# A transformer block's feed-forward layer: the last two of four batch elements with seven block products for eight in the first layer

## The chip, the cores and the metric

The kernel runs on one core of a Trainium2 chip. The metric is device time in microseconds, the median of three runs. The engines are TensorE (PE, with its weight loads as PEld), the vector engine (DVE), the scalar engine (ACT), GpSimd (POOL) and SyncE (SP), which issues all the DMAs here.

## The reference

Attention over chunks of 32 queries, each with its neighbours (16 to the left, 8 to the right) and 8 memory cells, then a feed-forward layer with a squared relu:

```python
for c in range(S // 32):                       # q, k, v: (4, 8, 768, 64)
    k_full, v_full = [mem_k, k[l:r]], [mem_v, v[l:r]]
    a = softmax(q_c @ k_full.T / sqrt(64))
    out[:, :, c] = a @ v_full
x = out.transpose(0, 2, 1, 3).reshape(3072, 512)
h = x @ w_in                                   # 512 x 2048
g = s * relu(h) ** 2 + b
y = g @ w_out                                  # 2048 x 512
```

All data are fp32, and w_in and w_out arrive as 64-bit words that the kernel rebuilds into fp32.

## The kernel before

The 3072 tokens are eight chunks of 384, two to a batch element (`NCHUNK`, `HALVES`). The 2048 hidden features are 16 slices of 128. A step `u` is one chunk with one slice (`STEPS`, line 100); there are 128. Chunks 0 and 1 share the first 32 steps, while the weights arrive; each later chunk has 16 steps of its own, and from step 40 on steps go in pairs.

Every operand of the two layers is held as a high and a low part of fp32r, and a product is three matmuls (high by low, low by high, high by high). `hidden` (line 720) makes a step of the first layer: 4 slices of the 512 input channels by 3 matmuls of 384 columns into one PSUM bank. Four scalar-engine passes follow in that bank: relu (736), square (737), affine with s and b (738) and the rounding to the high part (739); the vector engine subtracts it for the low part (740). `result` (line 743) makes a step of the second layer: three token tiles, three matmuls of 512 columns each (751), into three accumulator banks that a chunk holds for all its steps. The last step of a chunk copies them out (772, 774), and `ends` (781) does that for the last chunk, its last tile in two halves.

`attend(ch, d)` (539) makes attention for one half of a chunk's heads: loads (555, 562), scores (574), maximum, difference, exponential and sum (482 to 493), normalisation on POOL (500), transposes of 32 x 32 blocks on the vector engine (531, 32 to a half), products with v (588), and x's high and low parts (597, 598). From chunk 2 on, the values of one visit go on PE with the scores of the next, as one chain of instructions, for which four PSUM banks must be free.

`weight` (676) rebuilds one slice of w_in or w_out from a staging buffer of the ring `words` and splits it. All weights stay in SBUF afterwards: slices 0 to 7 in tiles of their own, 8 to 15 in tiles shared with the two layers' parts.

The order of all instructions is laid out before the run, by `Plan.lay` (201): each operation has a priority in step numbers (`anchor`, `H_AT`, `R_AT`, `FETCH`), a holding time (`HOLD`), and rings of buffers and banks (`Ring`, `room`, line 414) that it needs. Each engine then serves its list in this order, and waits by semaphores where an operand is late. `lock` keeps marked operations of the vector engine and POOL apart in that layout.

Of the kernel before, what the change touches and what calls it, by code (L numbers as in the profile page):

```python
# [60 lines left out]
BEFORE = 4.0  # L61
# [19 lines left out]
POOLED = set()  # L81
BANKS = 8
# [11 lines left out]
def G_AT(i, a):  # L94
# [4 lines left out]
PARTS = [0, 4, 10, NF]  # L99
STEPS = ([(ch, f) for lo, hi in zip(PARTS, PARTS[1:]) for ch in range(2) for f in range(lo, hi)]  # L100
         + [(ch, f) for ch in range(2, NCHUNK) for f in range(NF)])
FIRST = {}
for _u, (_, _f) in enumerate(STEPS):
# [8 lines left out]
            small=235, part=290, wide=1040, tiny=200, norm6=1000, norm3=650, mul6=470, mul3=270, issue=440)  # L112
# [4 lines left out]
CODE = dict(hidden=6, result=6, half=6, first=96, scores=96, value1=64, value2=32, scores1=96, scores2=96, turn=2, value=32)  # L117
# [55 lines left out]
class Plan:  # L173
# [27 lines left out]
    def lay(self, warm=None):  # L201
# [33 lines left out]
        while todo:  # L235
# [6 lines left out]
            for e in engines:  # L242
# [10 lines left out]
                put, got = [], None  # L253

                soon = min(((y[2].prio, y[1], y[0]) for y in waiting[e] if y[0] <= t + SOON[e]), default=None) if SOON[e] else None
                while ready[e]:
                    x = heapq.heappop(ready[e])
                    o = x[2]
                    if soon and soon[:2] < x[:2]:
                        put.append(x)  # L260
                        heapq.heappush(events, soon[2])
                        break
                    if e in pin and pin[e] is not o:
                        put.append(x)
                        continue
                    new = [v for v in o.vals if v.slot is None and v.ring.tiles is not None]
                    other = "POOL" if e == "DVE" else "DVE"
                    held = o.lock and e in lock and lock[other] > t

                    if o.lock and e in lock and free[other] <= t and any(y[2].lock and y[:2] < x[:2] for y in ready[other]):  # L270
                        put.append(x)
                        continue
                    given = []
                    for v in new if not held else ():
                        if not v.ring.can(v):
                            break
# [68 lines left out]
def body(ctx: ExitStack, tc: tile.TileContext, qkv, w1, w2, out):  # L345
# [30 lines left out]
    for i in range(NEARLY):  # L376
        early_tiles.append(at(WEIGHT_AT(0, 0), [P, SLOT], F32, name=f"early{i}", tag=f"slot{i}"))
        if i < 4:
            stat_tiles.append(tuple(at(top[0] % TURN_B, [QB, 2 * GB], F32, name=f"{n}{i}") for n in ("top", "den", "rden")))

    def weight_tile(half, f):
        late = f >= LATE_F
        if late and f not in wts:
            wts[f] = const.tile([P, SLOT], F32R, name=f"ww{f}", tag=f"slot{f - LATE_F}")
        if not late and (half, f) not in wts:
            place(WEIGHT_AT(half, f), 8 * DM)
            wts[half, f] = const.tile([P, 2, DM], F32R, name=f"w{half}_{f}", tag=f"w{half}_{f}")
        if not late:
            return wts[half, f]
        lo = half * (2 * DM + WEIGHT_AT(1, f) // 4)  # L390
        return wts[f][:, lo:lo + 2 * DM].rearrange("p (a n) -> p a n", a=2)

    xr = [[at(X_AT(i, a, d), [P, 2 * TOK], F32R, name=f"x{'HL'[a]}{d}_{i}") for a in range(2) for d in range(2)] for i in range(2)]
    gs = Ring([tuple(at(G_AT(i, a), [P, TOK], F32R, name=f"g{'HL'[a]}{i}") for a in range(2)) for i in range(3)])
    for half in range(2):
        for f in range(NF):
            weight_tile(half, f) if f < LATE_F else None
# [5 lines left out]
    words = ring("words", 3, [P, 2 * DM], F32)  # L403
    raws = ring("raw", 2, [P, QK], F32)
# [5 lines left out]
    outs = ring("partial", 2 * NT, [P, DM], F32)  # L410

    spare = [BANKS - 1]

    def room(r, kind):
        n = r.live.get
        if kind == "acc":
            r.free += spare
            spare.clear()
            return n("acc", 0) < NT
        few = sum(n(k, 0) for k in "stvSV")  # L420
        if kind in "SV":
            return few < 5 and r.next.get("v", 0) == len(r.vals["v"])
        if kind in "stv":
            return few < FEW if not r.next.get("acc", 0) else few < 3
        return n("h", 0) < 2
# [31 lines left out]
    def anchor(ch, d):  # L457
# [5 lines left out]
        return starts[ch] - JOIN - (8.0 if ch > NALONE else APART) * (2 - d)  # L463
# [3 lines left out]
    def xt(x, a, c):  # L467
        return x.tile[2 * a + c // 2][:, c % 2 * TOK:(c % 2 + 1) * TOK]
# [70 lines left out]
    def attend(ch, d):  # L539
# [5 lines left out]
        due = a + 2 if alone else anchor(ch, 2) if d else anchor(ch, 1)  # L545
# [32 lines left out]
        if d == 0:  # L578
            x_vals[ch] = Val(x_ring)
        x = x_vals[ch]  # L580
# [9 lines left out]
        def store(V):  # L590
            at = due + 0.9 if alone else due - 4
            for r in range(2):
                lo, hi = (0, 4 * QB) if r == 0 else (4 * QB, 6 * QB)
                to = lambda a, lo=lo, hi=hi: x.tile[2 * a + d][:, lo:hi]
# [22 lines left out]
        def soft(S):  # L617
            for n in range(2):
# [5 lines left out]
                if early:  # L624
                    turn(late, t, y, lambda m: t.parts.values(), (ch, d, n))
                else:
                    flip(a + BEFORE + n, t, y)
# [115 lines left out]
    def result(u):  # L743
# [3 lines left out]
        last = u + 1 == len(STEPS) or STEPS[u + 1][0] != ch  # L747

# [5 lines left out]
        for t in range(NT):  # L754
# [3 lines left out]
            if u + 1 == len(STEPS):  # L758
                ends(u, t, acc, products, (g["H"], g["L"], w["H"], w["L"]))
                continue  # L760
# [4 lines left out]
            if f < NF - 1 and o is None:  # L765
# [9 lines left out]
            if f < NF - 1:  # L775
                continue
# [4 lines left out]
    def ends(u, t, acc, products, reads):  # L781

        row = STEPS[u][0] * TOK + t * P
        cols = (0, DM) if t + 1 < NT else (0, DM // 2, DM)
        for i, (lo, hi) in enumerate(zip(cols, cols[1:])):
            o = Val(outs)
            op("PE", "result" if hi - lo == DM else "half", R_AT(u), lambda lo=lo, hi=hi: products(acc, t, lo, hi), (*reads, acc[0]), (acc[lo],))
            if (t + i) % 2:
                op("DVE", "out", u, lambda o=o, lo=lo, hi=hi: nc.vector.tensor_copy(o.tile[:, lo:hi], acc.tile[:, lo:hi]), (acc[lo],), (o[0],))
# [10 lines left out]
    for u, (ch, f) in enumerate(STEPS):  # L800
        if u == starts[ch]:
            plan.group = None
            for y in (ch, 0), (ch, 1), (ch + 1, 0):
                if y not in made and (y[0] == ch or NALONE <= ch < NCHUNK - 1):
                    made.add(y)
                    attend(*y)
            if ch == NCHUNK - 1:
                last_[3]()
        hidden(u)
        result(u)  # L810

    laid = plan.lay(warm)
    with tc.manual_schedule():
# [40 lines left out]
```

## Time and profile before

| | |
|---|---|
| runs | 601.72, 601.75, 602.56 us; median 601.75 |
| profiled execution, first to last instruction | 600.1 us; no other time is given for it |
| PE busy | 591.2 us (99%), 5052 instructions |
| weight loads busy | 528.9 us (88%) |
| vector engine busy | 333.5 us (56%) |
| scalar engine busy | 347.4 us (58%) |
| POOL busy | 24.2 us (4%) |
| HBM | 48.24 MB read, 6.29 MB written |

Busy time is the union of an engine's instructions. Matmuls overlap in the array and their ends are modelled, so the pace of a group is read from the starts of the groups, not from one matmul's duration. The profile's chain is found backward from the last instruction: at each step to what released it, or to the instruction before it on its engine.

### The profile page before, as it was taken

The page shows a single profiled execution, that of the slowest core. Times are in us where ns is not written, and L with a number is a line of the kernel's source. Part 1 is how long each engine was busy: PE and PEld are TensorE (multiplying, and loading weights), DVE is VectorE, ACT ScalarE, POOL GpSimd, SP SyncE. Part 2 cuts the span into 40 slices and gives each one's busy share as a digit, 9 for nine tenths or more (in the row PEclk, how much of TensorE's full clock was granted, in tenths as well). Part 3 has the DMA queues.
Part 4 walks back from the last instruction along what each step waited for, and adds up shares of the span by engine and source line. Part 5 has one row for each costly group of instructions (what it writes and reads, how often), then busy time and mean ns, then how long its engine had stood idle before and what let it go on. Part 6 is the DMA issues. An engine that isn't in the chain of part 4 may idle for free.

```text
span 600.1 us, 12337 instructions
## 1 busy us (share of the span) xinstructions
PE 591.2 (99%) x5052; PEld 528.9 (88%) x5057; DVE 333.5 (56%) x916; ACT 347.4 (58%) x743; POOL 24.2 (4%) x36
## 2 busy tenths in 40 slices
PE   8989999999999999999999999999999999999997
PEld 4778999989999999989989998998989989999996
DVE  4998999997381734728266371744628265121111
ACT  6999988855455546446445455546446545544553
POOL 1000000010010100001000010100001010000000
PEclk9999999999999999999999999999999999999999
DMA  8966644431230403103031210413013110010001
GB/s 341 416 237 217 196 147 168 143 134 53 68 118 1 134 0 131 55 13 121 0 133 54 73 61 1 133 54 131 2 31 114 42 56 1 1 52 1 0 2 53
DMA packets 17481, 55.32 MB, mean 92 GB/s; under 512 B 1936, under 2 KB 2192, under 8 KB 17424
## 3 DMA queue, kind: packets, MB, share of 16 engines
q1 hardware_dynamic: 17424, 54.53, 25.9%
q8 instruction: 39, 0.64, 0.4%
q14 instruction: 18, 0.15, 0.1%
HBM read 48.24 MB, written 6.29 MB: 91 GB/s over the span
## 4 chain that ended last, share of the span: by engine, by line
PE 93%; ACT 3%; DVE 2%; DMA 1%; issue 0%; SPq 0%; ACTq 0%
PE ps L728 44%; PE ps L751 43%; PE ps L588 4%; PE ps L574 3%; ACT t L486 1%; DMA early<-qkv 1%; DVE xL L598 0%; PE ps L516 0%; DVE wv L710 0%; ACT aT L525 0%; DVE t L498 0%; ACT wv L699 0%; DVE w L715 0%; ACT ps L738 0%; ACT w L705 0%
## 5 line engine op out<-in xcount | busy, mean ns | idle before, releaser
L740 DVE TENSOR_TENSOR gL<-ps,gH 128x384 fp32r<-128x384 f32 x128 | 71.2, 556 | 206.0 <-ACT gH L739 204.8
L736 ACT ACTIVATE ps<-ps 128x384 f32<-128x384 f32 x128 | 61.3, 479 | 173.7 <-PE ps L728 173.5
L728 PE MATMUL ps<-xH,w 128*128 128x384 f32 x512 | 130.5, 336 | 0.0
L728 PE MATMUL ps<-xH,ww 128*128 128x384 f32 x512 | 130.5, 336 | 0.0
L751 PE MATMUL ps<-ww,gH 128*128 128x512 f32 (+1 forms) x386 | 118.5, 389 | 0.0
L751 PE MATMUL ps<-w,gH 128*128 128x512 f32 x384 | 118.5, 390 | 0.0
L531 DVE STREAM_TRANSPOSE aT<-t 32x96 f32<-32x96 f32 x384 | 103.5, 270 | 6.1
L728 PEld LDWEIGHTS ps<-xH,ww 128*128 128x128 f32 x512 | 92.6, 188 | 1.3
L728 PEld LDWEIGHTS ps<-xH,w 128*128 128x128 f32 x512 | 92.7, 188 | 1.2
L728 PE MATMUL ps<-xL,w 128*128 128x384 f32 x256 | 87.2, 341 | 0.0
L728 PE MATMUL ps<-xL,ww 128*128 128x384 f32 x256 | 86.7, 339 | 0.0
L738 ACT ACTIVATE ps<-ps,b_sb,s_sb 128x384 f32<-128x384 f32 x128 | 82.5, 644 | 4.2
L751 PEld LDWEIGHTS ps<-ww,gH 128*128 128x128 f32 x386 | 72.4, 188 | 13.6
L751 PEld LDWEIGHTS ps<-w,gH 128*128 128x128 f32 x384 | 72.1, 188 | 13.6
L751 PE MATMUL ps<-w,gL 128*128 128x512 f32 x192 | 75.7, 394 | 0.8 <-DVE gL L740 0.8
L751 PE MATMUL ps<-ww,gL 128*128 128x512 f32 (+1 forms) x193 | 75.3, 390 | 0.0
L739 ACT ACTIVATE gH<-ps 128x384 fp32r<-128x384 f32 x128 | 62.9, 492 | 4.0
L737 ACT ACTIVATE ps<-ps 128x384 f32<-128x384 f32 x128 | 60.8, 475 | 4.1
L728 PEld LDWEIGHTS ps<-xL,w 128*128 128x128 f32 x256 | 48.2, 188 | 2.1
L728 PEld LDWEIGHTS ps<-xL,ww 128*128 128x128 f32 x256 | 48.2, 188 | 1.9
L751 PEld LDWEIGHTS ps<-w,gL 128*128 128x128 f32 x192 | 36.1, 188 | 7.7 <-DVE gL L740 1.5
L751 PEld LDWEIGHTS ps<-ww,gL 128*128 128x128 f32 x193 | 36.3, 188 | 6.2
(57 smaller groups left out, 415.1 us busy)
## 6 DMA issues: line engine op xcount, KB each, us to landing
raw<-qkv SPq DMA_DIRECT2D x28, 576.0 KB, 6.7
words<-w SPq DMA_DIRECT2D x24, 512.0 KB, 3.6
v<-qkv SPq DMA_DIRECT2D x28, 384.0 KB, 3.8
out<-partial SPq DMA_DIRECT2D x23, 256.0 KB, 2.0
early<-w SPq DMA_DIRECT2D x8, 512.0 KB, 10.2
early<-qkv SPq DMA_DIRECT2D x3, 576.0 KB, 6.1
early<-qkv SPq DMA_DIRECT2D x4, 384.0 KB, 9.7
early<-qkv SPq DMA_DIRECT2D x1, 577.0 KB, 3.6
```

Of the source, the lines that this page charges most:

```text
L486: op("ACT", "part", late + 0.2, lambda m=m: nc.scalar.activation(tv()[:, m, :], sv()[:, m, :], AF.Exp, bias=top()[:, m:m + 1], scale=SCALE ...
L531: nc.vector.transpose(aT.tile[rows, :, c, r * CHUNK:(r + 1) * CHUNK], t.tile[c * CHUNK:(c + 1) * CHUNK, r::2, g * CHUNK:(g + 1) * CHUNK])
L574: nc.tensor.matmul(S[n].tile[c * CHUNK:(c + 1) * CHUNK, (at * GB + j) * CELL:(at * GB + j + 1) * CELL], raw.tile[rows, k * CHUNK:(k + 1) * ...
L588: nc.tensor.matmul(to, vals_[half].tile[:, at:at + D], aT[n].tile[:, m, c, :], start=True, stop=True)
L728: nc.tensor.matmul(h.tile[:, :TOK], weight_tile(0, f)[:, wi, c * P:(c + 1) * P], xt(x, xi, c), start=(c == 0 and n == 0), stop=(c == NC_T ...
L736: op("ACT", "relu", u, lambda: nc.scalar.activation(hp(), hp(), AF.Relu), (), (h[0],))
L737: op("ACT", "square", u, lambda: nc.scalar.activation(hp(), hp(), AF.Square), (), (h[0],))
L738: op("ACT", "affine", u, lambda: nc.scalar.activation(hp(), hp(), AF.Identity, scale=s_sb, bias=b_sb), (c_s[0], c_b[0]), (h[0],))
L739: op("ACT", "high", u, lambda: nc.scalar.activation(g.tile[0], hp(), AF.Copy), (h[0],), (g["H"],))
L740: op("DVE", "low", u, lambda: nc.vector.tensor_tensor(g.tile[1], hp(), g.tile[0].bitcast(F32), ALU.subtract), (h[0], g["H"]), (g["L"],))
L751: nc.tensor.matmul(acc.tile[:, lo:hi], g.tile[gi][:, t * P:(t + 1) * P], weight_tile(1, f)[:, wi, lo:hi], start=(first and n == 0), stop=( ...
```

## The change

The steps of chunks 0 to 3 (elements 0 and 1) stay, 64 of them; the slices of chunk 3 go in another order (`LATER_F`). Elements 2 and 3 are made in 16 units (`unit`, `second`), eight to an element. A unit takes both token halves and two slices of the hidden features. Tokens, input channels and features are each cut in two, and the eight block products of the first layer become seven (`prod`), by the form of Strassen's scheme with shared sums. For it there are

- sums of the four parked x blocks (`sums`, `splits`): the attention of elements 2 and 3 leaves x in fp32 in four buffers (`park`, two scalar-engine copies a half in place of the split), three further sums and differences are made from them with one more buffer, and seven operands of 768 columns are split into high and low parts. They lie where slices 0 to 2, 6 and 7 of w_in and the two x tiles lay;
- mixed blocks of w_in (`mix`): for each of eight pairs of slices three operations of 512 and three of 256 columns, on the vector engine or, for pairs 1 and 3, POOL, then two splits of 512 columns and four writes to HBM. They have dates from step 30.82 to 61.59, and take the staging ring;
- loads of these blocks (`fetch`): 512 KB three times a unit and once every two units, into seven buffers that slices 8 to 14 of w_in held;
- the sums behind the products: three banks (kind L) take the products, of which one is used by products 0, 2, 4 and 6 in turn. Two of its states and one of another bank are saved by the scalar engine to SBUF; the vector engine adds them to a later bank (`hadd`) and squares the positive part (`hsq`); affine and high part stay on the scalar engine, the low part on the vector engine, now from SBUF;
- the second layer in two ways: the first token half accumulates in three banks over the eight units, the second half in banks of one unit each (kind r) that the vector engine adds to an SBUF buffer (`accum`).

The visits of attention for chunks 4 to 7 have dates of their own (`VISITS`), the transposes too (`FLIPS`). While a visit waits for its banks, no new bank of kind L or r is given out (`kept`).

```diff
+MIX = [30.82, 32.64, 34.69, 47.24, 47.55, 47.83, 61.59, 43.54]
+MIXENG = ['DVE', 'POOL', 'DVE', 'POOL', 'DVE', 'DVE', 'DVE', 'DVE']
+XENG = ['DVE', 'POOL', 'DVE', 'DVE']
+AHEAD = 0.88
+FLIPS = [5.12, 6.59, 6.68, 6.21, 6.01, 5.03, 6.84, 2.85, 10.89, 4.12, 6.97, 6.28]
+PROD = [-1.21, 1.4, 1.6, 1.68, 2.1, 3.33, 3.43]
+CHAIN = {'11': 2.04, '22': 0.52, '12': 3.22, '21': 4.37}
+SECONDS = [2.94, 3.55, 8.0, 3.91]
+XSUM = [-0.96, -0.62, 1.09, -0.07]
+XSPLIT = [-6.05, -2.28, -0.26, -2.49, 0.78, 0.92, -0.32]
+RBANKS = 2
...
 
 PARTS = [0, 4, 10, NF]
+NPLAIN = 2
+LATER_F = [3, 4, 5, 0, 1, 2, *range(6, NF)]
 STEPS = ([(ch, f) for lo, hi in zip(PARTS, PARTS[1:]) for ch in range(2) for f in range(lo, hi)]
-         + [(ch, f) for ch in range(2, NCHUNK) for f in range(NF)])
+         + [(2, f) for f in range(NF)] + [(3, f) for f in LATER_F])
+NPAIR = NF // 2
+NUNIT = (B - NPLAIN) * NPAIR
+UNIT = 3.75
+VISITS = [41.16, 48.0, 50.14, 54.14, 58.95, 69.41, 72.68, 81.06, 85.03]
+TURNED = set()
...
                     new = [v for v in o.vals if v.slot is None and v.ring.tiles is not None]
+                    if kept and any(v.kind in ("L", "r") for v in new):
+                        put.append(x)
+                        continue
                     other = "POOL" if e == "DVE" else "DVE"
                     held = o.lock and e in lock and lock[other] > t
...
+        if kind == "L":
+            return n("L", 0) < 3
+        if kind == "r":
+            return n("r", 0) < (RBANKS if r.next.get("r", 0) < len(r.vals["r"]) - NT else NT)
...
+    def sums(b):
+
+        at = AT(NPAIR * (b - NPLAIN))
+        plan.group = ("x", b)
+        full = lambda i: [c_park[i][r] for r in range(2)]
+        tt = lambda e, to, p, q, o: e.tensor_tensor(park(to), park(p), park(q), o)
+        firsts.append((b, 7, wide_op(XENG[0], "pre", at + XSUM[0], lambda e: tt(e, 4, 2, 3, ALU.add), (*full(2), *full(3)), full(4))))
+        wide_op(XENG[1], "pre", at + XSUM[1], lambda e: tt(e, 2, 0, 2, ALU.subtract), full(0), full(2))
+        splits(b, 0, 0, at + XSPLIT[0])
+        splits(b, 1, 1, at + XSPLIT[1])
+        wide_op(XENG[2], "pre", at + XSUM[2], lambda e: tt(e, 0, 4, 0, ALU.subtract), full(4), full(0))
+        splits(b, 2, 0, at + XSPLIT[2])
+        wide_op(XENG[3], "pre", at + XSUM[3], lambda e: tt(e, 1, 1, 0, ALU.subtract), full(0), full(1))
+        splits(b, 3, 4, at + XSPLIT[3])
+        splits(b, 4, 2, at + XSPLIT[4])
+        splits(b, 5, 1, at + XSPLIT[5])
+        splits(b, 6, 3, at + XSPLIT[6])
+
+    def splits(b, i, p, at):
+        src = [c_park[p][r] for r in range(2)]
+        firsts.append((b, i, op("ACT", "khigh", at, lambda: nc.scalar.activation(operand(i, 0), park(p), AF.Copy), src, (c_x[i]["H"],))))
+        firsts.append((b, i, op("DVE", "klow", at, lambda: nc.vector.tensor_tensor(operand(i, 1), park(p), operand(i, 0).bitcast(F32), ALU.subtract),
+                                (*src, c_x[i]["H"]), (c_x[i]["L"],), lock=True)))
...
+    def mix(j):
+
+        f1, f2 = 2 * j, 2 * j + 1
+        at = MIX[j]
+        plan.group = ("mix", j)
...
+        m = Val(words, "mix")
+        part = lambda lo, hi: m.tile[:, lo * DM // 2:hi * DM // 2]
+        two = lambda f, a: plain(f)[:, a, :].bitcast(F32)
+        e = MIXENG[j]
+        wide_op(e, "mix2", at, lambda e: e.tensor_tensor(part(0, 2), two(f2, 0), two(f2, 1), ALU.add), (w2v["H"], w2v["L"]), (m[0], m[1]))
+        wide_op(e, "mix2", at, lambda e: e.tensor_tensor(part(2, 4), two(f1, 0), two(f1, 1), ALU.add), (w1v["H"], w1v["L"]), (m[2], m[3]))
+        wide_op(e, "mix2", at, lambda e: e.tensor_tensor(part(2, 4), part(0, 2), part(2, 4), ALU.subtract), (m[0], m[1]), (m[2], m[3]))
+        wide_op(e, "mix1", at, lambda e: e.tensor_tensor(part(0, 1), part(1, 2), part(0, 1), ALU.subtract), (m[1],), (m[0],))
+        wide_op(e, "mix1", at, lambda e: e.tensor_tensor(part(1, 2), part(1, 2), part(2, 3), ALU.subtract), (m[2],), (m[1],))
+        wide_op(e, "mix1", at, lambda e: e.tensor_tensor(part(3, 4), part(2, 3), part(3, 4), ALU.subtract), (m[2],), (m[3],))
+        for h in range(2):
+            v = Val(words, "stage")
+            to = lambda a, v=v: v.tile.bitcast(F32R).rearrange("p (m a n) -> p a m n", m=2, a=2)[:, a]
+            fro = lambda h=h: m.tile.rearrange("p (m n) -> p m n", m=4)[:, (1, 0)[h]:(3, 4)[h]:(1, 3)[h], :]
+            need = [m[1], m[2]] if h == 0 else [m[0], m[3]]
+            op("ACT", "thigh", at, lambda to=to, fro=fro: nc.scalar.activation(to(0), fro(), AF.Copy), need, (v["H"],))
+            op("DVE", "tlow", at, lambda to=to, fro=fro: nc.vector.tensor_tensor(to(1), fro(), to(0).bitcast(F32), ALU.subtract), (*need, v["H"]), (v["L"],), lock=True)
+            op("SP", "issue", at, lambda v=v, h=h: nc.sync.dma_start(d_mixed[j][h].bitcast(F32), v.tile), (v["H"], v["L"]), (c_mixed[j][h][0],), size=P * TW * 4)
...
+    def fetch(k):
+
+        j, at = k % NPAIR, AT(k) - AHEAD
+        plan.group = ("fetch", k)
+        got = {}
+
...
+        load("mixed0", lambda: d_mixed[j][0], (c_mixed[j][0][0],), at + 1.1)
+        load("mixed1", lambda: d_mixed[j][1], (c_mixed[j][1][0],), at + 2.2)
+        if j % 2 == 0:
+            load("last", lambda: d_last[j // 2].rearrange("p a n -> p (a n)"), (c_last[j][0], c_last[j + 1][0]), at + 2.75)
+        else:
+            got["last"] = c_flow[k - 1]["last"]
...
+        def prod(i, bank, prio, start):
+            v, w = block(k, i)
+
+            def fn():
+                for c in range(2):
+                    for n, (wi, xi) in enumerate(((0, 1), (1, 0), (0, 0))):
+                        nc.tensor.matmul(bank.tile[:, :TOK], w(wi)[:, c * P:(c + 1) * P], operand(i, xi)[:, c * TOK:(c + 1) * TOK],
+                                         start=start and c == 0 and n == 0, stop=start and c == 1 and n == 2, skip_group_check=not start)
+
+            op("PE", "prod", at + prio, fn, (c_x[i]["H"], c_x[i]["L"], v[0]), (bank[0],))
+
+        def save(bank, prio):
+            v = Val(saves)
+            op("ACT", "save", at + prio, lambda: nc.scalar.activation(v.tile, bank.tile[:, :TOK], AF.Copy), (bank[0],), (v[0],))
+            return v
+
+        def chain(name, prio, bank, add):
+            h, g = Val(hs), Val(gs)
+            if add is None:
+                op("ACT", "hrelu", at + prio, lambda: nc.scalar.activation(h.tile, bank.tile[:, :TOK], AF.Relu), (bank[0],), (h[0],))
+                op("ACT", "hsquare", at + prio, lambda: nc.scalar.activation(h.tile, h.tile, AF.Square), (), (h[0],))
             else:
-                op("ACT", "store", u, lambda o=o, lo=lo, hi=hi: nc.scalar.activation(o.tile[:, lo:hi], acc.tile[:, lo:hi], AF.Copy), (acc[lo],), (o[0],))
-            op("SP", "issue", u, lambda o=o, lo=lo, hi=hi: nc.sync.dma_start(out[row:row + P, lo:hi], o.tile[:, lo:hi]), (o[0],), (), size=P * (hi - lo) * 4)
-
+                op("DVE", "hadd", at + prio, lambda: nc.vector.tensor_tensor(h.tile, bank.tile[:, :TOK], add.tile, ALU.add), (bank[0], add[0]), (h[0],))
+                op("DVE", "hsq", at + prio, lambda: nc.vector.scalar_tensor_tensor(h.tile, h.tile, 0.0, h.tile, ALU.max, ALU.mult), (), (h[0],), lock=True)
+            op("ACT", "haffine", at + prio, lambda: nc.scalar.activation(h.tile, h.tile, AF.Identity, scale=s_sb, bias=b_sb), (c_s[0], c_b[0]), (h[0],))
+            op("ACT", "hhigh", at + prio, lambda: nc.scalar.activation(g.tile[0], h.tile, AF.Copy), (h[0],), (g["H"],))
+            op("DVE", "hlow", at + prio, lambda: nc.vector.tensor_tensor(g.tile[1], h.tile, g.tile[0].bitcast(F32), ALU.subtract), (h[0], g["H"]), (g["L"],), lock=True)
+            return g
+
+        A = Val(ps, "L")
+        prod(0, A, PROD[0], True)
+        s1 = save(A, 0.1)
+        Bk = Val(ps, "L")
+        prod(1, Bk, PROD[1], True)
+        g11 = chain("11", CHAIN["11"], Bk, s1)
+        prod(2, A, PROD[2], False)
+        s2 = save(A, 1.2)
+        C = Val(ps, "L")
+        prod(3, C, PROD[3], True)
+        s5 = save(C, 1.7)
+        prod(4, A, PROD[4], False)
+        g22 = chain("22", CHAIN["22"], A, s5)
+        prod(5, C, PROD[5], False)
+        g12 = chain("12", CHAIN["12"], C, s2)
+        prod(6, A, PROD[6], False)
+        g21 = chain("21", CHAIN["21"], A, None)
+        return {(0, 0): g11, (0, 1): g12, (1, 0): g21, (1, 1): g22}
+
+    def second(k, gd):
+
+        b, j = NPLAIN + k // NPAIR, k % NPAIR
+        at = AT(k)
+        plan.group = ("second", k)
+
+        def mms(to, t, f, g, start, stop):
+            for n, (gi, wi) in enumerate(((1, 0), (0, 1), (0, 0))):
...
+        tail = k == NUNIT - 1
+        for q, prio in ((0, UNIT - 0.4 if tail else SECONDS[0]), (1, SECONDS[1])):
...
+
...
+            op("PE", "result2", at + SECONDS[2] + 0.3 * t, lambda r=r, t=t: [mm2(r, t, n) for n in range(2)], need[0] + need[1], (r[0],))
+            if j == 0:
+                op("ACT", "outcopy", at + SECONDS[3], lambda r=r, o=o: nc.scalar.activation(o.tile, r.tile, AF.Copy), (r[0],), (o[0],))
+            else:
+                op("DVE", "accum", at + SECONDS[3], lambda r=r, o=o: nc.vector.tensor_tensor(o.tile, r.tile, o.tile, ALU.add), (r[0],), (o[0],))
+            if j == NPAIR - 1:
...
+    for j in range(NPAIR):
+        mix(j)
+    for y in ((4, 1), (5, 0), (5, 1), (6, 0)):
+        attend(*y)
+    for k in range(NUNIT):
+        b, j = NPLAIN + k // NPAIR, k % NPAIR
+        fetch(k)
+        gd = unit(k)
+        second(k, gd)
+        y = {1: (2 * b + 2, 1), 3: (2 * b + 3, 0), 5: (2 * b + 3, 1), 7: (2 * b + 4, 0)}.get(j)
+        if y and y[0] < NCHUNK:
+            attend(*y)
+        elif b == B - 2 and j == 7:
...
+    plains = lambda *fs: using(*(c_w[0, f] for f in fs))
+    before_x = [plains(0, 1, 2)] * 2 + [plains(6, 7)] + [using(x_vals[0], x_vals[2])] * 2 + [using(x_vals[1], x_vals[3])] * 2
+    for b, i, o in firsts:
+        if b == NPLAIN:
+            later(o, before_x[i] if i < 7 else on(words) if i == 7 else plains(3, 4, 5))
+    for n in range(7):
+        hold(flows, n, plains(LATE_F + n))
+    gs.tiles.append(Lazy())
```

## Rows read from the trace of the kernel before

**Rows 1.** The page: busy time, PE's 40 slices, its clock, GB/s.

```profile
PE 591.2 (99%) x5052; PEld 528.9 (88%) x5057; DVE 333.5 (56%) x916; ACT 347.4 (58%) x743; POOL 24.2 (4%) x36
...
PE   8989999999999999999999999999999999999997
...
PEclk9999999999999999999999999999999999999999
...
GB/s 341 416 237 217 196 147 168 143 134 53 68 118 1 134 0 131 55 13 121 0 133 54 73 61 1 133 54 131 2 31 114 42 56 1 1 52 1 0 2 53
```

**Rows 2.** The page: the chain that ended last, by engine.

```profile
PE 93%; ACT 3%; DVE 2%; DMA 1%; issue 0%; SPq 0%; ACTq 0%
```

**Rows 3.** The chain in order of time: start us, us, what.

```profile
303.10 1.55 PE ps L588 x48
304.65 1.13 PE ps L574 x73
305.77 4.36 PE ps L728 x24
310.14 4.09 PE ps L751 x18
314.23 4.16 PE ps L728 x24
```

**Rows 4.** PE's waits: us in total, times, longest.

```profile
PE ps L751 <- DVE gL L740: 0.8, 1, 0.8
...
PEld ps L751 <- DVE gL L740: 1.5, 2, 1.1
```

**Rows 5.** Groups by line and shape: count, busy us, mean ns, idle before.

```profile
L531 DVE STREAM_TRANSPOSE aT<-t 32x96 f32<-32x96 f32 x384 | 103.5, 270 | 6.1
L738 ACT ACTIVATE ps<-ps,b_sb,s_sb 128x384 f32<-128x384 f32 x128 | 82.5, 644 | 4.2
L740 DVE TENSOR_TENSOR gL<-ps,gH 128x384 fp32r<-128x384 f32 x128 | 71.2, 556 | 206.0 <-ACT gH L739 204.8
L739 ACT ACTIVATE gH<-ps 128x384 fp32r<-128x384 f32 x128 | 62.9, 492 | 4.0
L736 ACT ACTIVATE ps<-ps 128x384 f32<-128x384 f32 x128 | 61.3, 479 | 173.7 <-PE ps L728 173.5
L737 ACT ACTIVATE ps<-ps 128x384 f32<-128x384 f32 x128 | 60.8, 475 | 4.1
L500 POOL TENSOR_TENSOR t<-t,rden 128x384 f32<-128x384 f32 x24 | 20.5, 854 | 444.4 <-DVE rden L496 269.3 <-ACT ps L737 120.9 <-ACT ps L738 54.2
L598 DVE TENSOR_TENSOR xL<-ps,xH 128x512 fp32r<-128x512 f32 x16 | 11.0, 689 | 31.7 <-ACT xH L597 31.7
L715 DVE TENSOR_TENSOR w<-wv,w 128x512 fp32r<-128x512 f32 x16 | 10.8, 684 | 2.7 <-ACT w L705 2.6
L705 ACT ACTIVATE ww<-wv 128x512 fp32r<-128x512 f32 x16 | 9.8, 628 | 2.4 <-DVE wv L712 2.4
L597 ACT ACTIVATE xH<-ps 128x512 fp32r<-128x512 f32 x16 | 9.6, 597 | 26.9 <-PE ps L588 25.9 <-PE ps L728 0.9
L774 DVE TENSOR_TENSOR partial<-ps,partial 128x512 f32<-128x512 f32 x12 | 7.9, 687 | 1.9 <-PE ps L751 1.8
L598 DVE TENSOR_TENSOR xL<-ps,xH 128x256 fp32r<-128x256 f32 x16 | 6.6, 412 | 0.0
L597 ACT ACTIVATE xH<-ps 128x256 fp32r<-128x256 f32 x16 | 6.1, 384 | 0.0
```

**Rows 6.** Three stretches: us, busy of each engine, clock, DMA share, GB/s.

```profile
55.00:160.00 105.00, 105.00 (x682) 95.28 (x679) 89.91 (x210) 78.66 (x151) 3.91 (x4) 1.00 0.41 136
170.60:314.20 143.60, 143.60 (x1249) 130.43 (x1249) 74.67 (x221) 72.98 (x145) 5.81 (x7) 1.00 0.20 67
339.00:375.00 36.00, 36.00 (x318) 32.73 (x320) 17.82 (x54) 18.11 (x36) 1.66 (x2) 1.00 0.17 56
```

**Rows 7.** DMA issues: KB each, median us to landing.

```profile
words<-w SPq DMA_DIRECT2D x24, 512.0 KB, 3.6
...
out<-partial SPq DMA_DIRECT2D x23, 256.0 KB, 2.0
```

**Rows 8.** Instructions in order of time, 314 to 597 us: start, us.

```profile
314.56 4.52 DVE L531 STREAM_TRANSPOSE aT<-t 32x96 f32<-32x96 f32 x16
314.67 0.83 POOL L500 TENSOR_TENSOR t<-t,rden 128x384 f32<-128x384 f32 x1 [4.57 <-DVE rden L496]
...
588.09 0.34 PE L728 MATMUL ps<-xL,ww 128*128 128x384 f32 x1
588.28 0.47 ACT L736 ACTIVATE ps<-ps 128x384 f32<-128x384 f32 x1 [3.98 <-PE ps L728]
...
596.94 0.42 DVE L789 COPY partial<-ps 128x256 f32<-128x256 f32 x1 [0.43 <-ACT partial L791]
```

More of the change, by code (lines that the diff above doesn't have):

```diff
@@ L116 @@
 RATE, LAND, NEAR, FAR = 408.0, 2150.0, 6, 3400.0
-CODE = dict(hidden=6, result=6, half=6, first=96, scores=96, value1=64, value2=32, scores1=96, scores2=96, turn=2, value=32)
+CODE = dict(prod=12, result2=12, hidden=6, result=6, half=6, first=96, scores=96, value1=64, value2=32, scores1=96, scores2=96, turn=2, value=32)
 BLOCK, SKEW = 256, 69
@@ L285, in lay @@
                         heapq.heappush(events, lock[other])
+                    elif any(v.kind in ("S", "V") for v in new):
+                        kept = True
                     put.append(x)
@@ L590, in store @@
         def store(V):
+            if ch >= HALVES * NPLAIN:
+                i = 2 * (ch % HALVES) + d
+                for r in range(2):
+                    lo, hi = (0, 4 * QB) if r == 0 else (4 * QB, 6 * QB)
+                    firsts.append((ch // HALVES, 8, op("ACT", f"park{r}", due - 4, lambda lo=lo, hi=hi, r=r: nc.scalar.activation(park(i)[:, lo:hi], V[r].tile[:, :hi - lo], AF.Copy),
+                       list(V[r].parts.values()), (c_park[i][r],))))
+                if i == 3:
+                    sums(ch // HALVES)
+                return
             at = due + 0.9 if alone else due - 4
@@ L747, in result @@
         last = u + 1 == len(STEPS) or STEPS[u + 1][0] != ch
+        final = last and (ch > 1 or f == NF - 1)
         def products(acc, t, lo=0, hi=DM):
@@ L778, in result @@
             op("SP", "issue", u, lambda ot=ot, row=row: nc.sync.dma_start(out[row:row + P, :], ot()), (o[0],), (), size=P * DM * 4)
[L781 to L789, printed above, removed]
-            else:
-                op("ACT", "store", u, lambda o=o, lo=lo, hi=hi: nc.scalar.activation(o.tile[:, lo:hi], acc.tile[:, lo:hi], AF.Copy), (acc[lo],), (o[0],))
-            op("SP", "issue", u, lambda o=o, lo=lo, hi=hi: nc.sync.dma_start(out[row:row + P, lo:hi], o.tile[:, lo:hi]), (o[0],), (), size=P * (hi - lo) * 4)
+    c_park = [fixed() for _ in range(5)]
@@ new lines, in body, with wide_op @@
+    c_x = [fixed() for _ in range(7)]
+    c_flow = {}
+    firsts = []
+    def wide_op(e, kind, prio, fn, reads, writes):
+        pool = e == "POOL"
+        return op(e, kind if pool else kind + "v", prio, lambda: fn(nc.gpsimd if pool else nc.vector), reads, writes, lock=True)
+    def sums(b):
[14 more added lines that the diff above has]
+        splits(b, 6, 3, at + XSPLIT[6])
@@ new lines, in splits @@
+    def splits(b, i, p, at):
[3 more added lines that the diff above has]
+                                (*src, c_x[i]["H"]), (c_x[i]["L"],), lock=True)))
+    c_first, c_last = [fixed() for _ in range(NPAIR)], [fixed() for _ in range(NPAIR)]
@@ L795, in body, with send, hold @@
+    def send(ch, t, o, at):
+        row = ch * TOK + t * P
+        op("SP", "issue", at, lambda: nc.sync.dma_start(out[row:row + P, :], o.tile), (o[0],), (), size=P * DM * 4)
+    o2 = {}
+    def hold(r, slot, ops):
+        ops = list(ops)
+        r.free = [x for x in r.free if x != slot]
+        v = Val(r, ("held", slot))
+        v.slot, v.left = slot, len(ops)
+        r.live["held", slot] = 1
+        for o in ops:
+            o.vals.append(v)
     made = {(0, 0), (0, 1)}
```

174 lines of the change are left out of this document (141 added, 33 removed).

## The prediction

> **What bounds the kernel now.** I read the page first. [...] A busy PE need not be a PE at its pace, so the chain of waits came next: 93% of it is PE, nearly all of that lines 728 (first layer) and 751 (second layer) [rows 2]. In order of time the chain shows the pace: 24 first-layer matmuls of 384 columns in 4.16 us (0.1733 each), then 18 second-layer matmuls of 512 columns in 4.09 us (0.2272 each), and the next group starts where the last one ends [rows 3]. A visit of attention costs 1.55 us for values, 1.13 for scores and 0.20 in the group behind it [rows 3]. PE waited for another engine's result in the second layer twice, 0.8 us in all [rows 4]. So time is the number of PE instructions by their pace, plus a head and a tail that the change leaves alone. What comes off PE comes off the span, as long as nobody makes PE wait.
>
> The profiled span is 600.1 us and the median of three runs 601.75, so 1.65 us lie around the span; the profile gives no other time for its execution. I sum on the span and add 1.65.
>
> **The change part by part.**
>
> *Fewer products.* Elements 2 and 3 have 64 steps with 12 first-layer matmuls each, 768. The new form has 16 units of 7 products with 6 matmuls each, 672. All are 384 columns wide, as before. 96 go: 96 x 0.1733 = 16.6 us. The second layer keeps 36 matmuls a unit (9 a step before), and the scores and values of all visits stay in number, so PE gains nothing to do. This bounds the gain: 600.1 - 16.6 = 583.5, and 585.1 with what lies around the span.
>
> [...]
>
> *The new elementwise work, in the units.* Before, a step has four scalar-engine passes (0.479, 0.475, 0.644, 0.492) and one vector subtraction (0.556) [rows 5]; a unit replaces four steps. A unit has on the scalar engine 3 saves, a relu, a square, 4 affines and 4 roundings: 4 x 0.479 + 0.475 + 4 x 0.644 + 4 x 0.492 = 6.9 us for 8.4 before. On the vector engine it has 3 additions, 3 squares, 4 subtractions (10 x 0.556) and 3 accumulations (0.687, line 774): 7.6 us for 2.2 before. A unit lasts 42 x 0.1733 + 36 x 0.2272 = 15.5 us on PE. The operations that read SBUF alone have no row of their size; below they cannot be free, and above I take the same width's rows with a PSUM operand.
>
> *Work per element on the vector engine.* One pair's mixing is 3 operations of 512 columns and 3 of 256, by lines 715 and 598 3 x 0.684 + 3 x 0.412 = 3.3 us, and two low parts, 1.4: 4.7 us. Six pairs mix there, 28 us; two pairs put the mixing on POOL, 3 x 1.14 + 3 x 0.57 = 5.1 us each by line 500's 0.854 for 384 columns, and 1.4 us of low parts on the vector engine. Operand sums and splits of 768 columns are 1.1 us each, 3 + 7 of them an element, in place of 8 x 1.1 us of x splits for both elements [rows 5].
>
> *Is the vector engine still beside PE?* Before, it is busy 74.7 of 143.6 us in element 1 (170.6 to 314.2) [rows 6]. Added: mixing 30.7; two more visits, as the new dates put six of them there for four. A visit costs 12.3 us: 17.8 us in a stretch with one visit (339 to 375), less eight 0.556 and the x split of 1.1 [rows 6]. Then three sums and five splits, 8.8, less three x splits, 3.3. That makes 135.5 us in 143.6 + 2 x 2.88 = 149.3: 91%. In element 2's units: 8 x 7.6 + 3 visits x 12.3 + a visit's transposes, 8.6, which the change dates 10.9 steps behind their visit + splits and sums, 13 = 120 us, in 8 x 15.5 + 3 x 2.88 + 1.75 = 134.1: 89%. Element 3 has no visit, 50%. Before, the stretch from 55 to 160 has it busy 89.9 of 105.0 us, 86%, with PE busy for all of it [rows 6]. So the cover holds at a load near to the new one; what it costs beyond is queueing. I charge 0.05 us a unit, 0.8 us.
>
> *The first transition.* Unit 0 needs operands whose sums go through one buffer of the weight staging ring, free only after the last mixing (due at step 61.59). From there: mixing 3.3, rounding and low parts 2.0 (0.63 and 0.684, twice 0.684), the write of 512 KB to HBM 3.6 (the landing of a load of this size; 256 KB written land in 2.0) [rows 7], two sums 2.2, rounding 1.0 and splitting 1.1, and some 0.2 in hand-overs: 13.4 us. Step 64 lies 2.41 steps x 4.126 = 9.9 us after 61.59, so product 2 is ready 3.5 us after it. PE has products 0 and 1 (2.1 us) and the results of steps 62 and 63 (4.1) for that. Hidden with 2.7 us to spare, if the vector engine, at 91%, takes each on its date; late by a visit's work before its transposes (12.3 less 8.6, 3.7 us) it costs 1.0, by two of them 4.7, by three 8.4. I take one, 1.0.
>
> *Visits among the units.* A visit's start wants four free banks; with three accumulators and bank A held, all others must drain. Between nothing and one uncovered bank gap (0.9 us, below) for each of four visits; I take 0.25 each, 1.0.
>
> *Fetches.* A unit reads 3.5 x 512 KB in 15.5 us, 118 GB/s, beside attention's loads; the first slice moved 341 and the second 416 GB/s [rows 1]. SP issues them in the same queue as loads and outputs, behind PE's release of a buffer, and seven buffers hold two units' blocks. Nothing.
>
> *Tail and head.* After the last product come relu to subtraction, 2.7 us, and PE has three result groups (3 x 2.05) in between; the last copy, 0.42 us before, becomes an addition on 256 columns (0.41) [rows 5, 8]. Nothing. The first 55 us have the same work, other dates for transposes come at step 18 and later: 0, give or take 0.5.
>
> Sum: 600.1 - 16.6 + 0.8 + 1.0 + 1.0 = 586.3, and with 1.65, 587.9 us.
>
> **The rivals.**
>
> *A. The vector engine becomes the bound.* If 86% is all that it can carry, element 1 takes 135.5/0.86 = 157.6 for 149.3 and element 2 120/0.86 = 139.5 for 134.1: 13.7 us late, 585.1 + 13.7 = 598.8. At 85% nothing of the gain is left. For: the queue is served in order, and the loads are above any shown. Against: sixteen transposes in a row kept it at 96% (16 x 0.27 in 4.52 us) [rows 5, 8], and in the 86% stretch it was not what PE waited for. Chance 0.08, of it 0.01 at no change and 0.01 slower.
>
> *B. POOL blocks it.* POOL's work in element 1 (two mixes 10.2, twelve normalisations 0.85 each) may stop the vector engine for its length: 135.5 + 20.4 = 155.9 for 149.3, 6.6 us late, 594.5. Sixteen transposes beside one POOL normalisation took 4.52 us, 0.28 each for 0.27 [rows 8], which speaks against it for operations with one input. [...] Chance 0.05.
>
> *C. The first transition is late* by two or three visits' work: 4.7 to 8.4 us for the 1.0 taken, 591.6 to 595.3. For: nine tenths of load and dates that fall together. Against: products 0 and 1 and all results of steps 62 and 63 are there to fill it. Chance 0.07.
>
> *D. Slower: PE waits inside the units.* Products 0, 2, 4 and 6 share one bank, each after a read of it. From the end of a hidden group's issue (588.09) to the scalar engine's start (588.28) it is 0.19 [rows 8]; with 0.479 for the save and 0.2 back, a gap is 0.87 us, 0.95 with the 0.556 addition: 2.7 us a unit. The unit saves 1.04. If more than 39% of the gaps lack other PE work, the kernel is slower; at half of them it is 587.9 + 16 x 1.35 = 609.5. Against: 18 or more result groups of 0.68 us lie between. For: the PE order is fixed beforehand, and with four result buffers they may not be ready. Chance 0.08.
>
> *E. The change doesn't do what it says* would need more PE work than counted; 42 matmuls a unit stand in the code. Chance 0.01, 601.8.
>
> **How the numbers follow.** Forecast 587.9 at 0.71, its own range 585 to 591. A 0.08, B 0.05, C 0.07, D 0.08, E 0.01. Lower end 584.8: no stall and half a us won at the head. Upper end 594.8 takes in B and most of C, some 0.82 in all. A measurement of this kernel tells 0.2% (1.2 us) from no change. Faster: 0.71 + 0.06 + 0.05 + 0.07 = 0.89; same 0.01 + 0.01 = 0.02; slower 0.01 + 0.08 = 0.09.
>
> **What would show it.** After: 672 matmuls of 384 columns in the units, at 0.173; PE's busy time down by 16 us, with idle of 1 to 4 us between step 64 and the end; the vector engine near 90% from 170 to 450. A is right if PE's waits name vector operations all through elements 1 and 2; B if vector operations grow beside POOL's; C if one wait of several us stands at the first product's operands; D if PE waits for saves in every unit. A time above 595 or under 584.5 would make the prediction wrong.

## The result, and the profile after

The changed kernel takes 592.24 us (median of 4 runs, 591.30 to 593.18) against 601.88 us before (4 runs, 601.72 to 602.56). The ratio is 0.9837, 95% interval 0.9823 to 0.9851: faster by 9.6 us, where the missing products are worth 16.6.

The page of the profile after, the rows that answer to [rows 1] and, of the chain, to [rows 2]:

```profile
span 590.7 us, 12521 instructions
...
PE 578.8 (98%) x4961; PEld 512.2 (87%) x4961; DVE 441.7 (75%) x1100; ACT 354.8 (60%) x735; POOL 41.7 (7%) x50
...
PE   9989999999999999999999999999999999999997
...
DVE  4988999787989887887888978697868543454443
...
PEclk9999999999999999999999999999999999999999
...
PE 84%; DVE 7%; DMA 5%; ACT 2%; issue 1%; DVEq 0%; SPq 0%; ACTq 0%
```

PE's share of the chain fell from 93% to 84%, and the vector engine's rose from 2% to 7%, the DMAs' from 1% to 5%. The slices do not tell where: those from 74 to 118 us show 9, and PE waited 0.7, 0.5 and 0.2 us in them. The chain in order of time (start us, us, what) shows the units first, as [rows 3] showed the steps:

```profile
461.09 4.16 PE ps L978 x24
465.25 2.05 PE ps L1028 x9
...
475.51 6.24 PE ps L978 x36
481.76 2.05 PE ps L1028 x9
483.81 1.04 PE ps L978 x6
484.85 1.37 PE ps L1054 x6
```

Line 978 is the seven products, 1028 and 1054 the second layer's two ways. 36 matmuls in 6.24 us are 0.1733 each, and each group starts where the last one ends. The groups are now 6 matmuls in places, and the pace is that of [rows 3]. From 165 to 590 us the profile lists no wait of PE. The seven products are as many as counted, 384 + 288 = 672:

```profile
L978 PE MATMUL ps<-x,ww 128*128 128x384 f32 x384 | 73.2, 336 | 0.0
...
L978 PE MATMUL ps<-home,ww 128*128 128x384 f32 x288 | 56.0, 336 | 0.0
```

The loss lies where the change was not looked for. From 80 to 165 us element 0 is still taking its weights. The chain there is PE from 99 to 116 us; before that, and from 116 to 163 us, it runs through other engines and DMAs. These are some of its pieces:

```profile
78.43 2.10 PE ps L819 x12
80.55 0.48 ACT ps L827
...
84.55 0.70 DVE wv L801
...
97.58 1.20 DVE partial L863 x2
98.78 0.48 DVE gL L831
99.30 2.34 PE ps L843 x9
...
123.03 4.99 DMA words<-w
128.04 0.43 DVE words L800
...
130.46 5.85 DMA words<-w
...
139.09 5.77 DMA words<-w
```

The lines 800 to 806 rebuild weights (709 to 715 before). In the first pieces PE waits for low parts (831) behind a full queue of the vector engine; in the later ones the chain runs through the rebuilding of weights, and that waits for the loads. The stretches (us, busy of PE, PEld, DVE, ACT, POOL, clock, DMA share, GB/s) say the same of after; two 20 us stretches first, then those that answer to [rows 6] and the two elements of units:

```profile
75.00:95.00 20.00, 19.28 (x98) 17.24 (x98) 19.38 (x47) 15.07 (x29) 0.00 (x0) 1.00 0.47 159
95.00:115.00 20.00, 19.30 (x96) 16.80 (x95) 17.57 (x37) 14.88 (x29) 0.00 (x0) 1.00 0.47 159
...
170.00:316.00 146.00, 146.00 (x1521) 132.18 (x1520) 119.73 (x352) 83.65 (x166) 18.39 (x19) 1.00 0.45 159
316.00:448.00 132.00, 132.00 (x1097) 119.39 (x1096) 107.30 (x274) 69.32 (x130) 9.24 (x9) 1.00 0.47 156
448.00:590.70 142.70, 138.85 (x698) 125.29 (x696) 69.75 (x122) 70.38 (x128) 0.00 (x0) 1.00 0.34 112
```

Before, the same two short stretches read:

```profile
75.00:95.00 20.00, 20.00 (x103) 18.21 (x102) 19.56 (x43) 17.33 (x34) 0.83 (x1) 1.00 0.49 159
95.00:115.00 20.00, 20.00 (x103) 18.24 (x102) 19.68 (x44) 16.79 (x33) 0.00 (x0) 1.00 0.49 159
```

So the vector engine was at 98% there already, without costing PE anything, and the average of 86% over 55 to 160 us in [rows 6] had hidden it. After, it does *less* in the second stretch (17.57 for 19.68), and PE is behind by then: something else holds the weights up.

To count the loss I took the start of each matmul to the next and subtracted the pace of its kind. From 80 to 180 us PE falls 7.2 us behind its pace after and 1.2 before, 6.0 more. (The 1.2 are two visits of attention: in each, before and after, the starts come 0.09 to 0.14 us late wherever the kind of matmul changes, 0.5 to 0.6 us in all.) By 55 us the changed kernel is 0.4 late. The rest of the span differs by half a us. Together that is about the 7.0 us that are missing (601.88 - 16.64 - 592.24 = -7.0).

What changed there shows in the instructions in order of time. SP's weight loads before (18 of them, the last one issued 0.33 us before the end of this line):

```profile
59.87 54.91 SPq L685 DMA_DIRECT2D words<-w  x18
```

After, on the vector engine and on SP:

```profile
54.04 0.69 DVE L922 TENSOR_TENSOR words<-home 128x512 f32<-128x512 f32 x1
...
139.09 0.33 SPq L776 DMA_DIRECT2D words<-w  x1
...
151.10 1.78 DVE L934 TENSOR_TENSOR words<-words,words 128x512 fp32r<-128x512 f32 x1
```

Line 922 is the first operation of the first pair's mixing. Its date is step 30.82, which is some 165 us, and it runs at 54: the date is only a priority, and the layout gives an idle engine any operation whose operands and buffers are there. It takes one of three staging buffers of `words`. To finish, the mixing needs a second buffer of the ring for each of its splits, and every weight has the earlier date; so the pair keeps its buffer until line 934's second subtraction ends at 152.9. The last weight load goes out at 139.1 us. Before, it was at 114.5 (59.87 + 54.91, less 0.33).

### The profile page after: what moved, and what is told of

Read it like the earlier page. It is cut to its first block, busy times and chain, and to the rows that moved or that the text cites. A ratio compares the mean times of both kernels' runs of the same rounds, so it can differ in the third digit from the quotient of the medians.

```text
span 590.7 us, 12521 instructions
## 1 busy us (share of the span) xinstructions
PE 578.8 (98%) x4961; PEld 512.2 (87%) x4961; DVE 441.7 (75%) x1100; ACT 354.8 (60%) x735; POOL 41.7 (7%) x50
## 4 chain that ended last, share of the span: by engine, by line
PE 84%; DVE 7%; DMA 5%; ACT 2%; issue 1%; DVEq 0%; SPq 0%; ACTq 0%
PE ps L978 20%; PE ps L843 17%; PE ps L819 17%; PE ps L1028 11%; PE ps L1054 11%; PE ps L670 4%; DMA words<-w 3%; PE ps L656 3%; DVE aT L613 2%; DMA raw<-qkv 2%; DVE wv L801 1%; DVE wv L803 1%; DVE partial L863 1%; PE ps L512 1%; ACT t L568 1%
## 5 line engine op out<-in xcount | busy, mean ns | idle before, releaser
L978 PE MATMUL ps<-x,ww 128*128 128x384 f32 x384 | 73.2, 336 | 0.0
L819 PE MATMUL ps<-x,ww 128*128 128x384 f32 x384 | 71.8, 338 | 1.3 <-DVE t L573 0.5
L819 PE MATMUL ps<-x,home 128*128 128x384 f32 x384 | 72.5, 338 | 0.0
L819 PEld LDWEIGHTS ps<-x,ww 128*128 128x128 f32 x384 | 66.9, 188 | 4.2 <-ACT gH L830 0.9
L819 PEld LDWEIGHTS ps<-x,home 128*128 128x128 f32 x384 | 66.9, 188 | 2.2
L978 PEld LDWEIGHTS ps<-x,ww 128*128 128x128 f32 x384 | 67.3, 188 | 1.0
L827 ACT ACTIVATE ps<-ps 128x384 f32<-128x384 f32 x64 | 30.7, 480 | 61.1 <-PE ps L819 60.7
L843 PE MATMUL ps<-ww,gH 128*128 128x512 f32 x192 | 59.4, 390 | 0.0
L843 PE MATMUL ps<-w,gH 128*128 128x512 f32 x192 | 59.3, 390 | 0.0
L978 PE MATMUL ps<-home,ww 128*128 128x384 f32 x288 | 56.0, 336 | 0.0
L996 ACT ACTIVATE words<-words,b_sb,s_sb 128x384 f32<-128x384 f32 x64 | 45.1, 705 | 11.7 <-DVE words L995 10.7
L978 PEld LDWEIGHTS ps<-home,ww 128*128 128x128 f32 x288 | 50.7, 188 | 1.6
L994 DVE TENSOR_TENSOR words<-ps,wv 128x384 f32<-128x384 f32 x48 | 26.7, 557 | 29.9 <-PE ps L978 29.4
```

The costliest lines, as they stand in the source:

```text
L819: nc.tensor.matmul(h.tile[:, :TOK], weight_tile(0, f)[:, wi, c * P:(c + 1) * P], xt(x, xi, c), start=(c == 0 and n == 0), stop=(c == NC_T ...
L827: op("ACT", "relu", u, lambda: nc.scalar.activation(hp(), hp(), AF.Relu), (), (h[0],))
L843: nc.tensor.matmul(acc.tile[:, lo:hi], g.tile[gi][:, t * P:(t + 1) * P], weight_tile(1, f)[:, wi, lo:hi], start=(first and n == 0), stop=( ...
L978: nc.tensor.matmul(bank.tile[:, :TOK], w(wi)[:, c * P:(c + 1) * P], operand(i, xi)[:, c * TOK:(c + 1) * TOK], start=start and c == 0 and n ...
L994: op("DVE", "hadd", at + prio, lambda: nc.vector.tensor_tensor(h.tile, bank.tile[:, :TOK], add.tile, ALU.add), (bank[0], add[0]), (h[0],))
L996: op("ACT", "haffine", at + prio, lambda: nc.scalar.activation(h.tile, h.tile, AF.Identity, scale=s_sb, bias=b_sb), (c_s[0], c_b[0]), (h[0],))
```

## The experiments

The theory (T1): the early mixing takes a third of the staging buffers, so the weights come by twos, and PE waits for the vector engine and the loads behind them. Rivals: the plain blocks' writes to HBM, as early, hold SP's queue (T2); the new dates of the transposes crowd the vector engine (T3).

**Mixing after the weights.** `made_w` are the operations that finish the 32 weight slices.

```diff
+        made_w = {o for w in c_w.values() for o in w["L"][1]}
-        wide_op(e, "mix2", ...)                       # the two first operations of a pair
+        wide_op(e, "mix2", ...).deps.update(made_w)
```

> The changed kernel, but no pair's mixing may be laid out before the last weight slice is rebuilt. Theory T1 (the first pair's mixing starts at 54 us, as soon as the vector engine has a free moment, and keeps one of the three staging buffers until 152 us, so the weights come in by twos instead of threes): the last weight load goes out at 115 to 120 us instead of 139, PE loses under 1 us between 80 and 165 us, and the time is 586.5 to 588.5 us. Rival T2 (the writes of w_in's blocks to HBM stand in SP's queue ahead of the weight loads and hold them up): 591 to 592.5 us, last load near 135 us. Rival T3 (the new dates of the transposes crowd the vector engine in the first 100 us): 591 to 592.5 us with the stalls at 85 to 100 us unchanged.

Measured: 588.36 us, ratio to before 0.9777 (0.9761 to 0.9794), 3.9 us under the changed kernel. The last weight load goes out as T1 said:

```profile
115.34 0.33 SPq L776 DMA_DIRECT2D words<-w  x1
```

From 80 to 100 us PE loses 0.2 for 2.6 us. T1 held in the load and, at its upper end, in the time. It missed in one thing: from 80 to 165 us PE loses 2.0 us more than in the kernel before, not under 1. One wait of 1.1 us for a low part stays at 123 us.

**Writes after the weights.**

```diff
-        op("SP", "issue", at, ... d_first[j] ...)     # and d_last
+        op("SP", "issue", at, ... d_first[j] ...).deps.update(made_w)
```

> The changed kernel, but the writes of w_in's plain blocks to HBM (512 and 256 KB a pair) are laid out only after the last weight slice is rebuilt; the mixing stays early. T1: one staging buffer is still gone, 591 to 592.5 us, weight loads still by twos, the last near 135 to 139 us. T2: 586.5 to 588.5 us, last weight load at 115 to 120 us. T3: 591 to 592.5 us.

Measured: 591.36 us, ratio 0.9827 (0.9813 to 0.9842), within the interval of the changed kernel. Mixing starts at 53.8 us, as early as in the changed kernel, and the last weight load goes out late:

```profile
136.95 0.33 SPq L776 DMA_DIRECT2D words<-w  x1
```

From 80 to 100 us PE loses 2.3 us. T2 alone is not the cause.

**Both.** The two edits together.

> Both the mixing and the plain writes only after the last weight slice. T1: as with the mixing alone, within 1 us. T2: as with the writes alone, within 1 us. If both hold weights up, it is the fastest of the three, near 586 us. T3: 591 to 592.5 us.

Measured: 586.73 us, ratio 0.9750 (0.9735 to 0.9764). It is 1.6 us under the first by the medians, a little more than T1 expected, near what was expected if both hold the weights up; the intervals touch. With the buffer back, the writes are worth something, about one us in PE's waits: 0.3 us up to 54 us, and the wait at 123 us is gone. What is left to the 585.1 that the products alone allow (601.76 - 16.64) is 1.6 us; by the starts of the matmuls 1.1 of it are two waits for low parts, at 145 and 177 us. T3 falls: with the transposes' dates untouched, the stretch that was bad reads as before the change, the vector engine at 98% and PE not waiting:

```profile
75.00:95.00 20.00, 20.00 (x103) 18.20 (x102) 19.56 (x42) 17.37 (x34) 0.83 (x1) 1.00 0.45 159
95.00:115.00 20.00, 20.00 (x104) 18.24 (x103) 19.80 (x42) 16.94 (x32) 0.00 (x0) 1.00 0.45 159
```

In order of time, SP's last weight loads with the plain blocks' writes behind them, and the second operation of the first pair's mixing:

```profile
106.48 8.39 SPq L776 DMA_DIRECT2D words<-w  x4
114.92 0.42 SPq L916 DMA_DIRECT2D first<-home  x1
...
129.85 0.68 DVE L924 TENSOR_TENSOR words<-home 128x512 f32<-128x512 f32 x1
```

**The kernel before with two staging buffers,** the other way round:

```diff
-    words = ring("words", 3, [P, 2 * DM], F32)
+    words = ring("words", 2, [P, 2 * DM], F32)
```

> The kernel before with two staging buffers for weights instead of three, nothing else. T1: the weights come in by twos as in the changed kernel, the last load near 139 us instead of 114, PE waits at 80 to 165 us for some 5 us, and the time is 605 to 609 us. T2 and T3: the third buffer is not what counts, 602 to 603 us.

Measured: 607.87 us, ratio 1.0099 (1.0084 to 1.0114), 6.1 us slower without any of the change. The weight loads end late here too, the last one issued at 135.8 us:

```profile
60.80 75.30 SPq L685 DMA_DIRECT2D words<-w  x19
```

PE loses 4.5 us between 80 and 100 us. T1 is shown from both sides.

The first run leaves one rival, which this one answers. The early mixing also takes 3.2 us of the vector engine between 54 and 73 us, just before the stretch that has no slack, and the dependency moves this work away together with the buffer. With two buffers and no mixing at all PE loses time at the same place, and more of it: the missing buffer is enough. What the 3.2 us add to it was not measured.

**Nothing on POOL.** In the version with both, some vector operations were long beside POOL (below).

```diff
-MIXENG = ['DVE', 'POOL', 'DVE', 'POOL', 'DVE', 'DVE', 'DVE', 'DVE']
-XENG = ['DVE', 'POOL', 'DVE', 'DVE']
+MIXENG = ['DVE'] * 8
+XENG = ['DVE'] * 4
```

> Built on the version with mixing and writes after the weights (586.7 us); all eight pairs' mixing and all operand sums on the vector engine, none on POOL. Beside POOL's mixing and normalisation some vector operations took up to 1.7 us instead of 0.16 to 0.7 (3.2 us in all in the changed kernel, 2.3 us in that version). If this blocking reaches PE, the time falls by 0.5 to 1 us, to some 586; if the vector engine's own load decides (two mixes and two sums move there, 13 us of work), it rises by 1 us or more; if both are covered, 586.2 to 587.4.

Measured: 586.25 us, ratio 0.9740 (0.9723 to 0.9758), the fastest kernel here, 1.0 us above the 585.3 that the products alone allow (601.91 - 16.64). From the version with mixing on POOL it can't be told apart: the intervals overlap. So the rise of 1 us or more did not come; between the other two expectations, which meet near 586.2, this run can't decide. Neither the load that moved nor the blocking cost anything that these runs can tell.

**A heavier vector engine in the units:** line `hlow` twice in each chain.

> Built on the same version; the subtraction for the low part of g is done twice in each chain of the units (64 more vector operations of 0.557 us, 35.6 us; the result is the same). The vector engine would be busy some 124 of 131 us (95%) in the third element instead of 106, and 87 of 143 in the fourth. If it becomes the bound at 86% as the prediction's rival A had it, the third element takes 144 us: 597 to 601 us. If the load itself is no bound as long as the order of its queue serves PE in time, 586.5 to 589 us.

Measured: 592.08 us, ratio 0.9831 (0.9816 to 0.9847), 5.3 us slower than its base for 35.6 us more work; between the two expectations, so neither held. The vector engine is busy 113.4 of 131 us in the third element. By the starts of the matmuls, two waits of PE at visits make 4.1 us of the loss (0.8 and 3.3), and the visit right behind the longer one takes 3.9 us for the 2.7 of the visit before it. The longer wait, on PE and on the vector engine (996 is the square there):

```profile
397.08 0.84 PE L1056 MATMUL ps<-w,ww 128*128 128x512 f32 x3
401.03 1.32 PE L979 MATMUL ps<-x,ww 128*128 128x384 f32 x6 [3.10 <-DVE words L995]
...
389.31 5.93 DVE L613 STREAM_TRANSPOSE aT<-t 32x96 f32<-32x96 f32 x21
...
398.81 1.13 DVE L613 STREAM_TRANSPOSE aT<-t 32x96 f32<-32x96 f32 x4
399.95 1.02 DVE L995 TENSOR_TENSOR words<-ps,wv 128x384 f32<-128x384 f32 x2
400.89 1.02 DVE L996 SCALAR_TENSOR_TENSOR words<-words 128x384 f32<-128x384 f32 x2
```

The addition that frees bank A (995) stands behind transposes and accumulations: from 386.6 to 401 us the chain runs through vector operations, none of which waits more than 0.03 us. So the load averaged over the element does not set the time. What does is a queue that is full for some 14 us, at a moment when PE has run out of other groups. Whether another order of that queue would save the wait at the same load was not tried.

**Two product banks.**

```diff
-            return n("L", 0) < 3
+            return n("L", 0) < 2
```

> Built on the same version; two banks instead of three may hold first-layer products at a time. If the chain through one bank (three gaps of 0.9 us a unit) is covered by the second layer's groups alone, 586.5 to 589 us. If the third bank is what covers the gaps, as the prediction's rival D would need, PE waits for saves and additions in every unit, 1 to 2.7 us a unit: 602 to 630 us.

Measured: 588.47 us, ratio 0.9776 (0.9761 to 0.9792), 1.7 us above its base by the medians; the intervals touch. One wait of 0.9 us for a save and a few tenths elsewhere; the second layer's groups cover the rest of the 16 units' gaps. The chain through one bank is no bound even so.

## Why the prediction was right, and where it was not

The time lay inside the outer range (584.8 to 594.8) and the direction was right; the forecast was 587.9 and the result 592.2. But that is outside the 585 to 591 of the main account, which had a chance of 0.71. The outer range reached so far up because it made room for rivals B and C, and neither of them is what happened: that the range held is luck. Two errors stand behind the number, of opposite sign, and they cancelled in part: 7.0 us were lost where the sum has nothing, and 2.8 us that it charges (0.8, 1.0 and 1.0) did not come.

- *Fewer products, 16.6 us*: right. 672 matmuls at 0.1733, and the version with everything after the weights stands 15.0 us under before (601.76 to 586.73), the one without POOL 15.7. PE's busy time fell by 12.4 us (591.2 to 578.8) for the 16 foreseen.
- *Tail and head, "Nothing"*: this is the step that failed, by 7 us. The first 55 us came out as said (0.4 late); from there to 170 us, the rest of element 0, the sum has no term at all, and 6.0 us were lost between 80 and 180. I took the dates of mixing and writes as the times at which they run, and looked for what is different in element 0 among the transposes alone. The layout is greedy: a date far ahead holds nothing back, and the first pair started mixing 110 us early and kept a staging buffer of the weights. What I ought to have asked of each new operation is not when it is due but from when its operands and buffers are there, and who else lives on these buffers.
- *The vector engine as cover*: too heavy by a tenth and harmless in the units. I had 91% and 89% for elements 1 and 2; it is 82% (119.7 of 146) and 81% (107.3 of 132), with the PE column full. The 0.8 us of queueing in the units did not come. The prices were near: line 998 and its like take 0.557 us, as put in, and the splits of 768 columns 0.95 for the 1.1 put in. Part of the surplus is that I added up durations: operations right behind one another overlap in the profile (above, two of line 995 take 1.02 us together and one 0.557). In the run with the low part twice, 63 more of 0.557 us raised the busy time by 29.9, 0.47 each.
- *The first transition, 1.0, and visits, 1.0*: neither shows. There is no PE wait from 312 to 340 us, and the visits cost their usual 0.5 to 0.6 us at the changes of matmul. The transition's chain of 13.4 us was built on the same error as the head, here to my favour. The last mixing, due at step 61.59, ten us before the units, had its first operation at 232 us and its last subtraction done at 241.6, some 70 us before them:

```profile
232.42 0.67 DVE L922 TENSOR_TENSOR words<-ww 128x512 f32<-128x512 f32 x1
...
240.31 1.29 DVE L934 TENSOR_TENSOR words<-words,words 128x512 fp32r<-128x512 f32 x2
```

- *Rivals.* A (bound at 86%) falls: the stretch at 98% in the kernel before, and the doubled low part, which cost 5.3 us and not 10 or more. That its "loads are above any shown" was a misreading: 98% stood in the trace. B: no run shows the vector engine stopped for all of POOL's work; beside POOL it lost a sixth of that price (3.2 us of the 20.4, last section), and no run could tell it from nothing in the time. C and D did not occur; D's gaps are covered even with two banks. The average over 105 us, on which A and the cover rested, is what kept me from seeing that element 0 had no slack to lose.
- *One reading was off, without effect on the sum.* [rows 4] has one wait of PE, 0.8 us; the two waits, 1.5 us in all, are those of the weight loads.

## What to carry to other kernels

Where a list scheduler lays out the order, a late date is not a gate: work that is added "later" starts as soon as an engine idles, and takes buffers from whoever needs them now. Give it a dependency, or buffers of its own; here the one on the mixing was worth 3.9 of the 7 us lost, and with the one on the writes 5.5. And read the load of an engine in stretches as short as the stage that has to be covered: 86% over 105 us was 98% over 40.

## What the runs showed of the hardware

Some vector operations between SBUF operands took longer beside a POOL operation, and ended 0.02 to 0.8 us after it. In the version with mixing and writes after the weights, on the vector engine and on POOL:

```profile
137.92 1.23 DVE L577 TENSOR_SCALAR den<-den 128x6 f32<-128x6 f32 x1
...
137.82 1.29 POOL L925 TENSOR_TENSOR words<-words 128x512 f32<-128x512 f32 x1
```

The first takes 0.16 us elsewhere; here it ends at 139.15, when POOL's ends at 139.11. In the changed kernel lines 806's and 934's subtractions took 1.30 and 1.78 for 0.69 us beside a pair's mixing on POOL, and POOL's line 923 took 1.74 for 1.29. In all it was 3.2 us of the vector engine's time, counted as what operations beside POOL took above the median of their kind. Transposes from SBUF were not longer: 16 of them, the first beside POOL's normalisation of 0.83 us, took 4.52 us, 0.28 each for a mean of 0.27 [rows 8]. That an operation on six columns with a single tensor operand (577 adds a constant) took 1.23 us for 0.16, I had not expected.

In the run with the low part twice, the granted clock (the third number from the end of a row) is 0.91 on average from 400 to 420 us, a stretch that begins inside PE's wait of 3.3 us, and 1.00 in the stretches on either side:

```profile
380.00:400.00 20.00, 17.92 (x87) 15.45 (x85) 17.96 (x54) 4.50 (x10) 1.84 (x2) 1.00 0.39 144
400.00:420.00 20.00, 18.97 (x222) 17.59 (x223) 17.15 (x42) 12.43 (x24) 1.85 (x2) 0.91 0.41 135
420.00:443.00 23.00, 23.00 (x155) 20.35 (x154) 20.26 (x49) 10.79 (x21) 0.71 (x1) 1.00 0.29 102
```

The visit of attention right behind the wait, in the stretch at 0.91, is the one that took 3.9 us for 2.7. How much of the 1.2 us the clock made was not shown.
